# One row-ordered array for attention outputs, and late row tiles on the GpSimd queue, in a kernel of two attention and two gMLP layers

## Chip, cores and metric

The kernel runs on one core of a Trainium2 chip. The metric is device microseconds (us) of one execution; the median of several executions is given. The profile is one more execution, recorded by the hardware profiler.

## What is computed

The input is one sequence of 2048 rows of 512 values in bf16. Four layers follow one another, each adding to the residual `x`: attention, gMLP, attention, gMLP, with the same weights both times.

```python
x = x + _A_ref(_layernorm(x), mem0, Wq, Wk, Wv, Wo, seg_len=32)
x = x + _B_ref(_layernorm(x), w_in, w_sp, b_sp, w_out)
...
# _A_ref: 64 segments of 32 rows, 32 heads of 128, one after the other
h = concat([mem, xs])                  # 8 memory rows and 32 rows
q, k, v = h @ Wq, h @ Wk, h @ Wv       # per head
o = softmax(mask(q @ k.T * scale)) @ v
o = o @ Wo                             # 40 rows of 512
mem = o[:8]; outs.append(o[8:])
...
# _B_ref
z = gelu(x @ w_in)                     # 2048 x 1376
z1, z2 = z[:, :688], layernorm(z[:, 688:])
g = w_sp @ z2 + b_sp[:, None]          # mixes all 2048 rows
return (z1 * g) @ w_out
```

A segment needs the memory rows of the one before it, so attention is a chain of 64 segments. The gMLP works on 16 row tiles of 128 rows; the product with `w_sp` (the gate) needs every row tile.

## The kernel before, in words

**Engines and queues.** TensorE (PE), VectorE (DVE) and ScalarE (ACT) run in the order in which the code names the operations (`ORDERED`, line 28); in the gMLP the same holds for SP, which only issues DMAs (line 216). GpSimd (POOL) and, in attention, SP get their order from the scheduler that builds the program. Every engine's queue is served in order: an instruction that waits holds up those behind it. Each DMA is issued by the queue of one engine.

**Attention** (`a_block`, line 453). `segment` (line 610) projects Q, K and V, forms the scores and the weighted sums, and closes with `wo_pass` (line 547), 128 matmuls into `pw`. `pw` holds 32 rows: the 8 memory rows for the next segment and the first 24 output rows. The last 8 output rows of a segment are computed apart, for 16 segments at once (`wo_last`, line 556; `y_part`, line 565), into `pwB`. So there are two arrays in DRAM: `oA_d` (one slab per segment, written by `store_o`, line 605) and `oB_d` (one slab per 16 segments, line 579 and, after the last segment, line 804). `store_o` runs for all 65 products.

**Rows** (`_Rows`, line 139). When a row tile's attention output is complete, `y_load` (line 172) loads the residual and, by eight small DMAs, the outputs from both arrays; `y_add` (line 185) adds and stores the new residual to `xd`; `y_stats` and `y_norm` (line 193) normalise it and store it as bf16 to `xb_d`. All these stores are on SP's queue. Attention does this for row tiles 0 to 11, one per segment, as soon as they are complete, on DVE. Row tiles 12 to 15 need the last `wo_last`, so the gMLP does them: the late rows. `late_load` (line 239) loads them on POOL's queue and adds on POOL; `late_norm` (line 248) does their statistics and normalising on DVE, with its own Newton steps for the reciprocal root (`_rstd_dve`, line 116: three steps, a dozen tiny operations). `apply` (line 153) prepares a row tile for attention: it normalises, stores to `xn_d`, and loads the result back in eight pieces, on SP's queue.

**gMLP** (`b_block`, line 202). First the projection stage: for each row tile `project` (line 259) runs 12 matmuls of `xnT` (transposed by a DMA from `xb_d`, line 237, three buffers) with `w_in_sb` into one of two PSUM buffers `pz`; ACT takes GELU of both halves (lines 266, 267), DVE the statistics of the second half (269 to 271). After every odd tile DVE does Newton's steps for the pair (line 294), and after the next even tile ACT normalises both (line 274). After tile 5 and tile 9 `late_norm` runs ahead of the pair's Newton steps (line 287), and the loads of tiles 14 and 15 follow tile 5. SP's queue has the transposes of `xnT`, of `w_sp` (three ahead, line 257) and the stores of the late rows.

Then the gate stage, lines 354 to 364: for each output tile `gate` runs 32 matmuls (16 row tiles, two halves) into `pg`, in the same PSUM buffers; `product` (DVE, line 321) multiplies by `z1`; `turn_u` transposes on PE and `finish` multiplies by `w_out`, adds the residual, and in the first gMLP takes the statistics for the next attention and calls `apply` for row tiles 0 and 1. `turn_u` and `finish` of one tile stand inside the gate of the next:

```python
for t in range(NT):
    gate(t, range(0, 6))
    if t > 0:
        turn_u(t - 1)
    gate(t, range(6, 12))
    if t > 0:
        finish(t - 1)
    gate(t, range(12, NT))
    product(t)
```

**Memory.** The pools of a layer lie one behind the other in SBUF in the order of the code, and the next layer's pools take the same addresses: a tile can be written when the tiles that lay there have been read for the last time. In the gMLP `w_in_sb` comes first; at these addresses attention has `hA`, `KA`, `QQ` and `uT`, used until its last segment. `xnT` lies in the pool `b_z` (line 212).

Of the kernel before, what the change touches and what calls it, by code (L numbers as in the profile page):

```python
# [138 lines left out]
class _Rows:  # L139


    def __init__(self, nc, pool, xd, xn_d, xb_d, oA_d, oB_d, x_in):
# [47 lines left out]
    def y_stats(self, tb, MV):  # L190
        _stats(self.nc, self.pool, self.y[tb][0], MV[:, tb, :])

    def y_norm(self, tb, MV, RS):
# [3 lines left out]
        self.nc.vector.tensor_scalar(out=_nat(xn[:]), in0=_perm(o), scalar1=MV[:, tb, 0:1], scalar2=RS[:, tb:tb + 1],
                                     op0=ALU.subtract, op1=ALU.mult)
        self.nc.sync.dma_start(self.xb_d[tb * P:(tb + 1) * P, :], xn[:])


def b_block(tc, c, rows, xd, MV_in, RS_in, MV_out, RS_out, w_in, w_sp, w_out, S, first, out_final=None):
# [641 lines left out]
```

## Time and profile before

| | before |
|---|---|
| median of 3 runs | 1998.38 us (1998.09 to 2000.65) |
| the profiled execution's own time | 1993.78 us |
| span in its trace, first to last instruction | 1992.1 us |
| PE busy | 1787.7 us (90%) |
| DVE busy | 1259.4 us (63%) |
| ACT busy | 1050.9 us (53%) |
| POOL busy | 138.2 us (7%) |
| mean granted clock of PE | 0.97 |

The span lies within the execution's time. Busy times are of the span; matmuls overlap, so a busy PE is not PE at its peak. [...] The first gMLP lies at about 800 to 1018 us, the second at about 1781 to 1992 us.

### The profile page before, as it was taken

To read this page: it belongs to the slowest core of one execution; us is meant where nothing else is said; L and a number is where in the kernel's file an instruction comes from. 1 tells how busy PE (TensorE), PEld (TensorE's weight loads), DVE (VectorE), ACT (ScalarE), POOL (GpSimd) and SP (SyncE) were. 2 spreads that over 40 slices of the span, in tenths; PEclk is the share of its full clock that TensorE was granted. 3 is DMA by queue.
4 is the path that set the end of the run, shared out by engine and by line. 5 is a ranking of instruction groups with operands and counts; after the bars stand their busy time and mean duration, and the time that the engine had idled before them with its cause. 6 is when DMAs were issued, how large, how long until landed. Compare 5 with 4: busy or idle time off the path is not lost.

```text
span 1992.1 us, 94947 instructions
## 1 busy us (share of the span) xinstructions
PE 1787.7 (90%) x43776; PEld 1033.7 (52%) x43776; DVE 1259.4 (63%) x2876; ACT 1050.9 (53%) x1880; POOL 138.2 (7%) x287
## 2 busy tenths in 40 slices
PE   3899999999999999657989999999999999985798
PEld 1555555555555555324645555555555555542355
DVE  2666777777777767353346677667777776665422
ACT  1566666666666665341236666666666666643311
POOL 5000000000000000320010000000000000004000
PEclk8999999999999999878999999999999999997899
DMA  9100000120012001435640000001200210033363
GB/s 348 31 20 18 19 17 17 32 65 26 17 40 64 19 15 47 131 82 123 157 136 24 20 22 20 21 20 57 63 21 24 79 50 15 9 115 100 86 140 101
DMA packets 179935, 120.08 MB, mean 60 GB/s; under 512 B 117280, under 2 KB 156976, under 8 KB 179536
## 3 DMA queue, kind: packets, MB, share of 16 engines
q1 hardware_dynamic: 158864, 70.43, 13.7%
q0 software_dynamic: 9376, 28.88, 4.2%
q10 hardware_dynamic: 11296, 14.70, 2.5%
q8 instruction: 342, 5.60, 1.1%
q14 instruction: 57, 0.47, 0.1%
HBM read 59.29 MB, written 33.69 MB: 47 GB/s over the span
## 4 chain that ended last, share of the span: by engine, by line
PE 39%; DVE 7%; ACT 5%; issue 2%; DMA 2%; POOL 1%; SPq 0%; DVEq 0%; POOLq 0%; ACTq 0%
PE psm L494 12%; PE pg L313 7%; PE pw L551 5%; PE psb L494 4%; DVE KA L631 2%; PE py L338 2%; ACT rows L627 2%; PE psO L674 2%; ACT E L655 2%; PE pwB L560 2%; PE psS L651 1%; DVE E L658 1%; PE psM L718 1%; PE psD L727 1%; PE pT L329 1%
## 5 line engine op out<-in xcount | busy, mean ns | idle before, releaser
L494 PEld LDWEIGHTS <-hA 128*32 128x32 bf16 x12288 | 308.9, 96 | 308.2 <-DVE hA L603 48.5
L627 ACT CAST rows<-psm 128x512 bf16<-128x512 f32 x512 | 300.6, 587 | 189.9 <-PE psm L494 189.9
L551 PE MATMUL pw<-Wo_sb,uT 128*32 128x128 bf16 x16640 | 265.5, 219 | 28.0 <-issue 19.7
L494 PE MATMUL psm<-Wq_sb,hA 128*32 128x512 bf16 x4096 | 273.5, 383 | 13.8 <-DVE hA L603 12.8
L551 PEld LDWEIGHTS <-uT 128*32 128x32 bf16 x16640 | 244.4, 97 | 67.6 <-issue 29.6
L494 PE MATMUL psm<-Wk_sb,hA 128*32 128x512 bf16 x4096 | 270.0, 381 | 0.0
L494 PE MATMUL psv<-Wv_sb,hA 128*32 128x512 bf16 x4096 | 268.2, 382 | 0.0
L631 DVE STREAM_TRANSPOSE QQ<-rows 128x512 bf16<-128x512 bf16 x256 | 182.1, 711 | 89.1 <-ACT rows L627 87.8
L690 DVE TENSOR_TENSOR uT<-psO,Rt 128x384 bf16<-128x384 f32 x256 | 138.1, 539 | 126.1 <-ACT Rt L680 126.1
L631 DVE STREAM_TRANSPOSE KA<-rows 128x512 bf16<-128x512 bf16 x256 | 182.0, 711 | 38.6 <-ACT rows L627 33.1
L655 ACT ACTIVATE E<-psS 128x448 bf16<-128x448 f32 x256 | 140.3, 548 | 107.5 <-PE psS L651 107.5
L637 DVE CAST VA<-psv 128x512 bf16<-128x512 f32 x256 | 175.7, 686 | 2.3 <-PE psv L494 0.2
L313 PE MATMUL pg<-z2n,wspT 128*128 128x344 bf16 x1024 | 164.8, 314 | 12.0 <-ACT z2n L274 7.1
L263 PE MATMUL pz<-w_in_sb,xnT 128*128 128x512 bf16 (+1 forms) x384 | 92.6, 409 | 74.2 <-DMA xnT<-xb_d 53.5
L596 POOL COPY QQ<-QTB 128x256 bf16<-128x256 bf16 x128 | 51.5, 403 | 1408.0 <-PE psS L651 847.1
L651 PEld LDWEIGHTS <-KA 128*64 128x64 bf16 x2048 | 79.8, 113 | 127.9 <-DVE KA L631 127.5
L680 ACT ACTIVATE Rt<-Rt 128x1024 f32<-128x1024 f32 x128 | 135.6, 1059 | 4.0
L313 PEld LDWEIGHTS <-wspT 128*128 128x128 bf16 x1024 | 96.4, 99 | 67.6 <-issue 14.7
L679 ACT ACTIVATE Rt<-psD 128x1024 f32<-128x1024 f32 x128 | 129.0, 1008 | 0.0
L494 PEld LDWEIGHTS <-hB 128*32 128x32 bf16 x3072 | 76.5, 97 | 101.0 <-issue 32.5
L735 DVE TENSOR_TENSOR uT<-psO,Rm 128x128 bf16<-128x128 f32 x256 | 62.8, 286 | 92.5 <-PE psO L674 82.3
L651 PE MATMUL psS<-QQ,KA 128*64 128x80 bf16 x2048 | 109.9, 208 | 10.3
(116 smaller groups left out, 2268.5 us busy)
## 6 DMA issues: line engine op xcount, KB each, us to landing
oA_d<-o_sb SPq DMA_DIRECT2D x130, 64.0 KB
Wo_sb<-in_A_Wo_dram POOLq DMA_DIRECT2D x8, 1024.0 KB, 13.4
xs<-xd ACTq DMA_DIRECT2D x32, 256.0 KB
xd<-y_o SPq DMA_DIRECT2D x28, 256.0 KB
y_o<-oA_d SPq DMA_DIRECT2D x96, 48.0 KB
Wq_sb<-in_A_Wq_dram POOLq DMA_DIRECT2D x8, 512.0 KB, 7.0
Wk_sb<-in_A_Wk_dram POOLq DMA_DIRECT2D x8, 512.0 KB, 11.0
xn_d<-ln_xn SPq DMA_DIRECT2D x32, 128.0 KB
```

Of the source, the lines that this page charges most:

```text
L263: nc.tensor.matmul(pz[:, c0:c1], lhsT=xnT[tt][:, kt, :], rhs=w_in_sb[:, kt, c0:c1], start=(kt == 0), stop=(kt == KT - 1))
L313: nc.tensor.matmul(pg[t][:, k, 0:344], lhsT=wsp[t][:, st, :], rhs=z2n[:, st, 344 * k:344 * k + 344], start=(st == 0), stop=(st == NT - 1))
L494: nc.tensor.matmul(ps[32 * cg:32 * cg + 32, :], lhsT=lhs(kt, cg), rhs=rhs(kt, cg), start=(kt == 0), stop=(kt == KT - 1), tile_position=(0, ...
L551: nc.tensor.matmul(po[32 * cg:32 * cg + 32, 0:128], lhsT=lhs[:, n, :], rhs=wo_rhs(h, cg), start=(h == 0), stop=(h == H - 1), tile_position ...
L627: nc.scalar.copy(r[:], ps[:])
L631: nc.vector.transpose(out=QQ[:, j % 2, :, 0:32] if j < 2 else KA[:, j % 2], in_=r[:])
L637: nc.vector.tensor_copy(VA[:, r].rearrange("p i e -> p (i e)"), ps)
L651: nc.tensor.matmul(pS[64 * g:64 * g + 64, i, c0:80 if K is KA else 112], lhsT=K[:, r, n:n + 2, :].rearrange("p h k -> p (h k)"), rhs=q if ...
L655: nc.scalar.activation(out=E[:, r], in_=pS, func=ACT.Exp, scale=scale)
L679: nc.scalar.activation(out=o, in_=in_, func=ACT.Ln)
L680: nc.scalar.activation(out=o, in_=o, func=ACT.Exp, scale=-1.0)
L690: nc.vector.tensor_tensor(out=hview(uT_nxt, 2 * r, 2 * r + 2, 8, 32), in0=oview(2 * r, 2 * r + 2, 8, 32), in1=Rr[:, :, :, 0:24], op=ALU.mult)
```

## The change

The two arrays become one, `o_d`, whose row M + r (M = 8) is output row r: a segment's product is stored as 32 consecutive rows, the 8 memory rows landing where `store_last` later writes the last 8 output rows of the segment before. `y_load` is then one DMA for the residual and one for the outputs. The product of segment 0 has nothing to store and isn't. In attention the tiles `oB`, `VB`, `KTB` and `QTB` become two fixed buffers each, used in turn, and come first in memory: index 0 of all four, then index 1. In the gMLP `xnT` gets a pool of its own right behind `w_in_sb`; the two together take 14,080 bytes a partition, the four tiles of index 0 take 14,336.

The stores of the late rows, of row tile 11, of the last `o_d` rows and the DMAs of `apply` in the first gMLP are issued on POOL's queue instead of SP's. Tiles 12, 13 and 14 are loaded ahead of the projections and tile 15 after tile 5. The two late tiles share the Newton steps of the projection pair (four columns instead of two and two), after which come their `y_norm`. The gate stage begins with 14 of 16 steps for output tiles 0 and 1, then the last two steps of each; later gates are cut at 8 and 13 instead of 6 and 12.

```diff
     def apply(self, tb, MV, RS, first=False, x=None, eng=None):
+        eng = eng or nc.sync
...
-        nc.sync.dma_start(self.xn_d[M + tb * P:M + (tb + 1) * P, :], xn[:])
+        eng.dma_start(self.xn_d[M + tb * P:M + (tb + 1) * P, :], xn[:])
...
     def y_load(self, tb, first, eng, x=None, o=None):
...
-        ot = o.rearrange("p (cg c) -> p cg c", cg=4)
-        for j in range(4):
-            eng.dma_start(ot[32 * j:32 * j + 24], self.oA_d[4 * tb + j + 1].rearrange("(cg r) c -> r cg c", cg=4)[8:32])
-            r0 = 32 * (tb % 4) + 8 * j
-            eng.dma_start(ot[32 * j + 24:32 * j + 32], self.oB_d[tb // 4, r0:r0 + 8, :].rearrange("r (cg c) -> r cg c", cg=4))
+        eng.dma_start(o, self.o_d[M + tb * P:M + (tb + 1) * P, :])
...
-    def y_add(self, tb, first, eng):
+    def y_add(self, tb, first, eng, store):
...
-        self.nc.sync.dma_start(self.xd[tb * P:(tb + 1) * P, :], o)
+        store.dma_start(self.xd[tb * P:(tb + 1) * P, :], o)
...
         wp = ctx.enter_context(tc.tile_pool(name="b_w", bufs=1))
+        xp = ctx.enter_context(tc.tile_pool(name="b_x", bufs=3))
...
-            xnT[tt] = zp.tile([P, KT, P], BF16, name="xnT", bufs=3)
+            xnT[tt] = xp.tile([P, KT, P], BF16, name="xnT")
...
-            rows.y_add(tb, first, nc.gpsimd)
+            rows.y_add(tb, first, nc.gpsimd, nc.gpsimd)
...
+        def norms(q, late):
+            n = 4 if late else 2
+            for k, tb in enumerate(late):
+                rows.y_stats(tb, mv[q][:, 2 + k, :])
+            rs[q] = zp.tile([P, 4], F32, name="rs")
+            nb[q] = zp.tile([P, 2], F32, name="nb")
+            _rstd_dve(nc, zp, rs[q][:, 0:n], mv[q][:, 0:n, 1], n)
+            nc.vector.scalar_tensor_tensor(out=nb[q][:], in0=mv[q][:, 0:2, 0], scalar=-1.0, in1=rs[q][:, 0:2], op0=ALU.mult, op1=ALU.mult)
+            for k, tb in enumerate(late):
+                rows.y_norm(tb, mv[q][:, 2 + k, 0:1], rs[q][:, 2 + k:3 + k], nc.gpsimd)
...
-        for tb in (NT - 4, NT - 3):
-            late_load(tb)
+        late_load(NT - 4)
+        late_load(NT - 3, gp.tile([P, DM], F32, name="xs")[:], gp.tile([P, DM], F32, name="xo", bufs=1)[:])
+        late_load(NT - 2, gp.tile([P, DM], F32, name="xs")[:], rows.pool.tile([P, DM], F32, name="ln_x")[:])
...
-            if tt in (5, 9):
-                late_norm(NT - 4 + 2 * (tt // 9))
-            if tt == 5:
-                for tb in (NT - 2, NT - 1):
-                    late_load(tb)
...
+                norms(tt // 2, {5: (NT - 4, NT - 3), 9: (NT - 2, NT - 1)}.get(tt, ()))
             elif tt > 1:
                 normalise(tt - 2)
                 normalise(tt - 1)
+            if tt == 5:
+                late_load(NT - 1)
...
-                rows.apply(t, MV_out, RS_out, x=xo[:])
+                rows.apply(t, MV_out, RS_out, x=xo[:], eng=nc.gpsimd)
...
+        gate(0, range(0, NT - 2))
+        gate(1, range(0, NT - 2))
+        gate(0, range(NT - 2, NT))
+        product(0)
+        gate(1, range(NT - 2, NT))
+        turn_u(0)
+        product(1)
+        gate(2, range(0, 6))
+        finish(0)
+        gate(2, range(6, 8))
+        for t in range(2, NT):
+            if t > 2:
+                gate(t, range(0, 8))
+            turn_u(t - 1)
+            gate(t, range(8, 13))
+            finish(t - 1)
+            gate(t, range(13, NT))
             product(t)
...
+        for i in range(2):
+            oBr[i] = pers.tile([P, H, P], BF16, name=f"oB{i}")
+            VBr[i] = pers.tile([P, 2, 4, DH], BF16, name=f"VB{i}")
+            KTBr[i] = pers.tile([P, 2, 16, 32], BF16, name=f"KTB{i}")
+            QTBr[i] = pers.tile([P, 2, 16, 32], BF16, name=f"QTB{i}")
...
+        def store_last(G, eng):
+            eng.dma_start(o_d[M + 512 * G:M + 512 * G + 512, :].rearrange("(j r) d -> j r d", r=32)[:, 24:32, :], yB.pop(G)[:])
...
-            nc.sync.dma_start(oA_d[s], o_sb[:])
+            eng.dma_start(o_d[SEG * (s - 1):SEG * s, :].rearrange("r (cg c) -> cg r c", cg=4), o_sb[:])
...
-            store_o(s, pw)
+            if s > 0:
+                store_o(s, pw, nc.sync)
...
-        store_o(NSEG, pw)
+        store_o(NSEG, pw, nc.gpsimd)
...
-        nc.sync.dma_start(oB_d[NB // 4 - 1], yl[:])
+        store_last(NB // 4 - 1, nc.gpsimd)
...
-        y_add(ys[0])
+        y_add(ys[0], nc.gpsimd)
         run(copies)
-        rows.y_norm(ys[0], MV_out, RS_out)
+        y_norm(ys[0], nc.gpsimd)
```

## Rows read from the trace of the kernel before

**Rows 1.** Windows: us, busy and (count) of PE, PEld, DVE, ACT, POOL; clock; DMA.
```profile
60.00:800.00 740.00, 706.10 (x20406) 417.37 (x20402) 540.32 (x1175) 459.60 (x831) 24.60 (x61) 1.00 0.10 30
811.00:892.50 81.50, 44.89 (x192) 20.43 (x193) 41.19 (x168) 32.75 (x46) 25.86 (x41) 0.77 0.39 100
888.00:892.00 4.00, 4.00 (x22) 1.92 (x20) 2.38 (x12) 3.29 (x5) 0.00 (x0) 1.00 0.66 140
1791.00:1875.00 84.00, 47.34 (x193) 21.27 (x194) 41.84 (x171) 32.73 (x46) 26.18 (x41) 0.74 0.39 98
1895.00:1982.00 87.00, 87.00 (x572) 52.05 (x571) 21.13 (x26) 11.01 (x26) 0.00 (x0) 1.00 0.53 126
```

**Rows 2.** PE's longest wait, 60 to 800 us: total, times, longest.
```profile
PE pw L551 <- issue: 6.4, 16, 0.8
```

**Rows 3.** What PE waited for, 800 to 1020 us: total, times, longest.
```profile
PE pz L263 <- DMA xnT<-xb_d: 26.3, 2, 17.1
PE pz L263 <- ACT z L267: 6.7, 2, 6.1
PE pg L313 <- DMA wspT<-in_B_w_sp_dram: 4.9, 2, 4.2
```

**Rows 4.** Timeline of PE, first gMLP: start, us, line, operation, count, [idle before].
```profile
803.61 7.08 PE L560 MATMUL pwB<-Wo_sb,oB 128*128 128x512 bf16 x32
814.57 8.81 PE L263 MATMUL pz<-w_in_sb,xnT 128*128 128x512 bf16 x36 [3.88 <-issue]
832.67 11.18 PE L263 MATMUL pz<-w_in_sb,xnT 128*128 128x512 bf16 x48 [9.28 <-DMA xnT<-xb_d]
866.34 11.41 PE L263 MATMUL pz<-w_in_sb,xnT 128*128 128x512 bf16 x48 [17.06 <-DMA xnT<-xb_d]
...
1012.04 1.34 PE L313 MATMUL pg<-z2n,wspT 128*128 128x344 bf16 x8
```

**Rows 5.** Timeline of the SP queue, first gMLP.
```profile
829.94 12.81 SPq L237 DMA_TRANSPOSE xnT<-xb_d  x6
...
863.33 0.33 SPq L188 DMA_DIRECT2D xd<-xo  x1
863.75 8.25 SPq L237 DMA_TRANSPOSE xnT<-xb_d  x4
```

**Rows 6.** Timeline of POOL (GpSimd), first gMLP.
```profile
824.07 1.17 POOL L187 TENSOR_TENSOR y_o<-y_o,y_x 128x512 f32<-128x512 f32 x1
...
862.15 1.15 POOL L187 TENSOR_TENSOR xo<-xo,xs 128x512 f32<-128x512 f32 x1 [1.65 <-DMA xo<-oA_d]
```

**Rows 7.** Timeline of ACT (ScalarE), first gMLP.
```profile
810.73 0.59 ACT L803 COPY yB<-pwB 128x512 f32<-128x512 f32 x1 [6.75 <-PE pwB L560]
...
888.55 0.72 ACT L266 ACTIVATE z<-pz 128x688 f32<-128x688 f32 x1
...
892.96 1.81 ACT L274 ACTIVATE z2n<-z,NBz,RSz 128x688 bf16<-128x688 f32 x2 [1.11 <-DVE NBz L295]
894.68 0.72 ACT L266 ACTIVATE z<-pz 128x688 f32<-128x688 f32 x1
```

**Rows 8.** Timeline of DVE (VectorE), first gMLP.
```profile
823.77 1.50 DVE L127 TENSOR_TENSOR nq<-nq,nt 128x2 f32<-128x2 f32 x1
...
845.10 0.70 DVE L135 BATCH_NORM_STATS2 bnst<-y_o 128x6 f32<-128x512 f32 x1
...
847.14 0.17 DVE L119 TENSOR_SCALAR nt<-MV 128x2 f32<-128x2 f32 x1
```

**Rows 9.** DMA issues: count, KB each, median us from issue to landing.
```profile
y_x<-xd POOLq DMA_DIRECT2D x2, 256.0 KB, 3.1
```

**Rows 10.** Timeline of PE, second gMLP.
```profile
1781.60 8.77 PE L560 MATMUL pwB<-Wo_sb,oB 128*128 128x512 bf16 x32
...
1888.79 3.09 PE L313 MATMUL pg<-z2n,wspT 128*128 128x344 bf16 x20
...
1982.91 1.34 PE L313 MATMUL pg<-z2n,wspT 128*128 128x344 bf16 x8
```

More of the change, by code (lines that the diff above doesn't have):

```diff
@@ L177, in y_load, with y_stats, y_norm, b_block @@
         eng.dma_start(x, (self.x_in if first else self.xd)[tb * P:(tb + 1) * P, :])
-        ot = o.rearrange("p (cg c) -> p cg c", cg=4)
-        for j in range(4):
-            eng.dma_start(ot[32 * j:32 * j + 24], self.oA_d[4 * tb + j + 1].rearrange("(cg r) c -> r cg c", cg=4)[8:32])
-            r0 = 32 * (tb % 4) + 8 * j
-            eng.dma_start(ot[32 * j + 24:32 * j + 32], self.oB_d[tb // 4, r0:r0 + 8, :].rearrange("r (cg c) -> r cg c", cg=4))
+        eng.dma_start(o, self.o_d[M + tb * P:M + (tb + 1) * P, :])
         self.y[tb] = (o, x)
-    def y_add(self, tb, first, eng):
+    def y_add(self, tb, first, eng, store):
         o, x = self.y[tb]
         eng.tensor_tensor(out=_perm(o) if first else o, in0=_perm(o) if first else o, in1=_nat(x) if first else x, op=ALU.add)
-        self.nc.sync.dma_start(self.xd[tb * P:(tb + 1) * P, :], o)
-    def y_stats(self, tb, MV):
-        _stats(self.nc, self.pool, self.y[tb][0], MV[:, tb, :])
-    def y_norm(self, tb, MV, RS):
+        store.dma_start(self.xd[tb * P:(tb + 1) * P, :], o)
+    def y_stats(self, tb, mv):
+        _stats(self.nc, self.pool, self.y[tb][0], mv)
+    def y_norm(self, tb, mean, rstd, store):
         o, _ = self.y.pop(tb)
         xn = self.pool.tile([P, DM], BF16, name="ln_xn", bufs=2)
[L197 to L202, printed above, removed]
+        self.nc.vector.tensor_scalar(out=_nat(xn[:]), in0=_perm(o), scalar1=mean, scalar2=rstd, op0=ALU.subtract, op1=ALU.mult)
+        store.dma_start(self.xb_d[tb * P:(tb + 1) * P, :], xn[:])
+def b_block(tc, c, rows, xd, MV_out, RS_out, w_in, w_sp, w_out, S, first, out_final=None):
     nc = tc.nc
@@ L225, in b_block @@
         w_out_sb = mid.tile([P, 6, DM], BF16, name="w_out_sb")
-        MVz = mid.tile([P, NT, 2], F32, name="MVz")
-        RSz = mid.tile([P, NT], F32, name="RSz")
-        NBz = mid.tile([P, NT], F32, name="NBz")
-        xt, xnT, z2, wsp = {}, {}, {}, {}
+        xt, xnT, z2, wsp, mv, rs, nb = {}, {}, {}, {}, {}, {}, {}
         def load_x(tt):
@@ L397 @@
     xb_d = dram.tile([S, DM], BF16, name="xb_d")
-    oA_d = dram.tile([S // SEG + 1, P, P], F32, name="oA_d")
-    oB_d = dram.tile([S // 512, P, DM], F32, name="oB_d")
+    o_d = dram.tile([M + S, DM], F32, name="o_d")
     rp = ctx.enter_context(tc.tile_pool(name="rows", bufs=1))
-    rows = _Rows(nc, rp, xd, xn_d, xb_d, oA_d, oB_d, x_in)
+    rows = _Rows(nc, rp, xd, xn_d, xb_d, o_d, x_in)
     with tc.manual_schedule(engines=ORDERED):
@@ L503, in a_block @@
             nc.gpsimd.memset(t[:], 0.0)
-        oA_d, oB_d, maskM = rows.oA_d, rows.oB_d, c["maskM"]
+        o_d, maskM = rows.o_d, c["maskM"]
         blk_state = {}
@@ L578, in out, with y_add, y_norm @@
                 if q == 3:
-                    nc.sync.dma_start(oB_d[G], yB.pop(G)[:])
+                    store_last(G, nc.sync)
             adds.append(out)
             yield
-        def y_add(tb):
-            rows.y_add(tb, first, nc.vector)
-            rows.y_stats(tb, MV_out)
+        def y_add(tb, store):
+            rows.y_add(tb, first, nc.vector, store)
+            rows.y_stats(tb, MV_out[:, tb, :])
             copies.append(lambda: _rstd_act(nc, RS_out[:, tb:tb + 1], MV_out[:, tb, 1:2], c))
+        def y_norm(tb, store):
+            rows.y_norm(tb, MV_out[:, tb, 0:1], RS_out[:, tb:tb + 1], store)
         seg_state = {}
@@ L618, in segment @@
             if s % 16 == 0:
-                oBs[tb // 4] = blkp.tile([P, H, P], BF16, name="oB")
+                oBs[tb // 4] = oBr[tb // 4 % 2]
             oB = oBs[tb // 4]
@@ L786, in tail @@
                 if ys:
-                    rows.y_norm(ys.pop(0), MV_out, RS_out)
+                    y_norm(ys.pop(0), nc.sync)
                 if tb % 4 == 3 and j4 == 0 and tb > 4:
```

56 lines of the change are left out of this document (18 added, 38 removed).

## The prediction

> **What bounds the kernel now.** I read the windows first, then who waits for whom, then the timelines of single engines around the places where TensorE (PE) stands still. In the attention blocks PE is busy 706.1 of 740 us at full clock [rows 1]; the longest entry in its waits there is 6.4 us, in pieces under 1 us, and none ends on a DMA [rows 2]. The last part of each gMLP is as dense: 87.0 of 87 us [rows 1]. Between them lies the projection stage (16 row tiles, 12 matmuls each). There PE is busy 44.9 of 81.5 us in the first gMLP and 47.3 of 84 in the second, at mean granted clocks of 0.77 and 0.74 [rows 1]. So some 165 us of 1992 are badly used, and nearly all that the change can win lies there and at its two ends. The list of waits names what PE lacks: 26.3 us on transposed inputs `xnT`, 6.7 on its PSUM buffers (which ScalarE empties), 4.9 on `wspT` [rows 3]. The timeline has the same as holes: 3.88 us ahead of the first projection, 9.28 ahead of the fourth tile, 17.06 ahead of the tenth [rows 4]. SP's own timeline gives the reason: the transposes stand in its queue behind the store `xd<-xo` of a late row tile and leave 0.4 us after it, at 863.75 [rows 5]. That store waits for GpSimd's add, which started at 862.15 after a wait for its loads [rows 6]. Tiles that have nothing to do with the late rows are held up by queue order alone.
>
> **What limits the stage once SP is free.** Two row tiles then form a loop: ScalarE's GELU of the odd tile, VectorE's statistics and Newton steps, ScalarE's two normalisations, the next odd tile. The undisturbed pair runs from 888.55 to 894.68: 6.13 us, of which 4.41 to the first normalisation [rows 7]. PE's work for a tile is 8x512 + 4x352 = 5504 columns; at the 0.221 us per 512 columns of the product before it (7.08 us for 32) [rows 4] that is 2.38 us, 4.76 us for a pair. So PE fits in at full clock, which it had from 888 to 892 [rows 1] while this loop ran.
>
> **The change, part by part.**
> First weights and `xnT` over dead tiles, last read in segment 60 of 0 to 63. Both can land before attention ends. The first projection then needs only the PSUM of the last product, free when ScalarE's copy ends, 810.73 + 0.59 = 811.32 [rows 7]. First GELU: 811.32 + 2.38 = 813.7, since the product leaves the clock full.
> Stores of late rows on GpSimd's queue. SP keeps transposes alone: the 9.28 and 17.06 us go. Late next is the loop of pairs: GELU of tile 1 at 813.7 + 2.38 = 816.1, and seven pairs of 6.13 us bring tile 15 to 859.0.
> Newton shared. Each of the two late pairs still lays its statistics on the loop, 845.10 to 847.14 = 2.04 us [rows 8], 4.1 in all, but no second chain of Newton steps. Their normalising passes follow it, beside ScalarE's normalisations: nothing. So 863.1.
> GpSimd's adds stay. The one at 824.07 took 1.17 us [rows 6], and a 2-element VectorE operation over it took 1.50 us [rows 8]. Four a block cost from 0 to 4 x 1.2 = 4.8 us, according to how many meet Newton steps; I take two, 2.4 us, as three of them follow close on each other at the first steps: tile 15 at 865.5. [...]
> GpSimd's queue now holds the last output store, the two stores of tile 11, two `w_out` loads, 8 late loads instead of 36, 4 adds, 8 late stores; in the first gMLP also the 18 DMAs that prepare the next attention's first two tiles, ahead of its `Wo` loads. Only late rows and that preparation stand behind its waiting instructions. A load of 256 KB lands in 3.1 us [rows 9], taken for the stores too. The last output, copied at 811.3, can be read at 815; three loads and adds end at about 823, and statistics want tile 12 at 830. Tile 15 (buffers free at 835, two stores and two loads issued at 0.6 each, 3.1, 1.2) is ready at 842, wanted at 845. Tile 14's input is tight: normalising 0.7, store 0.6 + 3.1, transpose 2.6 (863.75 [rows 5] to the matmul at 866.34 [rows 4]), 7.0 us, against 1.8 + 6.13 + 1.3 - 2.4 = 6.8 until PE wants it. Cost 0 to 2 us; I take 0, because 3.1 is for twice a bf16 tile's bytes.
> Gate order. Fourteen of the sixteen steps of the first two gates now come before the last two normalisations are needed: 28/32 of two gates at 6.72 - 1.74 = 4.98 (below), 8.7 us of PE work. Tile 15 is normalised 4.41 + 1.81 us after its GELU starts [rows 7], so it is covered; without that cover up to 6 us a block would return. The first gate starts with the last GELU, or up to 6.13 - 1.4 - 2.38 = 2.4 us ahead of it: I take 1, so 864.5.
> Gate stage. From the second gate's end to the last one's are 14 periods, 1982.91 - 1888.79 [rows 10], 6.72 us each. Sixteen, less the one turn and output product that the first lacks (3840 of 14848 columns, 1.74 us), plus 0.5 for a first product on VectorE, are 106.3 us. The `wspT` waits go, since 9 DMAs for each of the next attention's first tiles leave SP.
> Output array. Nine loads a tile become two, 130 small stores 128. SP gives up time that PE never waited for: nothing, bounded by 3 us either way. Fixed buffers, the store left out, small statistics tiles: nothing, they stand beside PE's 95% in attention.
>
> **The sum.** First gMLP: the last gate ends at 864.5 + 106.3 = 970.8 instead of 1012.04 + 1.34 = 1013.4 [rows 4]: 42.6 us. Second: the product ends at 1781.60 + 8.77 = 1790.4; copy 0.6, then 2.4 to the first GELU, 51.8 to the last (2.4 + 42.9 + 4.1 + 2.4), less 1, and 106.3 bring the last gate to 1950.5 instead of 1984.25 [rows 10]: 33.8 us, as its gates had run without waits. Together 76.4. The profiled execution took 1993.78 us, 1.7 more than its span; 1917.4 follows. The median shown, 1998.38, lies 4.6 above that execution, so I forecast **1922 us**.
>
> **Rivals.**
> *Late rows still come late.* GpSimd's queue is served in order; a store of tile 12 behind a waiting load, or slower landings, would hold `xnT` of tiles 14 and 15. For: no slack at tile 14. Against: tiles 12, 13 and 15 have 3 us or more. A hole like the 9.28 us one a block: about 10, so 1942. [...]
> *PE stays at the lower clock.* For: means of 0.74 and 0.77 [rows 1]. Against: the long holes explain them, and 888 to 892 has 1.00. A tile would take 4.76 us, the stage 76 instead of 53: 23 us a block lost, 1968.
> *The early loads are not early.* If `w_in` and `xnT` stay behind the end of attention in their queues, the first projection starts as now: about 5 us a block, 1932.
> *Slower.* The single array joins stores and wide loads in SP's queue: a segment's store waits for a load of rows, a load for the last store, and the `pre` inputs behind them arrive late. It decides from 76/128 = 0.6 us a segment; at 0.8 us the time is 1922 + 102 = 2024. Against: fewer instructions in that queue, and no PE wait on it now [rows 2].
>
> **From this to the numbers.** Forecast 0.70, late rows 0.13, low clock 0.08, loads not early 0.06, slower 0.03. A time within 0.2% (4 us, about what a measurement of this kernel tells from no change) needs gains and losses that cancel: 0.01, out of the forecast's share. Low end: no add blocks (-4.8), gates start early (-2.8), the median lies no higher than the profiled execution (-4.6), SP gives 3: 1907. High end: every add blocks (+4.8) and the late rows' case: 1946. Low clock, slower and the tails lie outside.
>
> **What would show it.** Right: no PE hole above 2 us between the last output product and the first gate; odd GELUs 6.1 us apart, about 8 where late statistics stand; clock 1.00 there; the first projection within 1 us of ScalarE's copy; no PE wait on `wspT`; attention as long as before. Wrong: holes on `xnT` at tiles 12 to 15 (late rows), matmuls at twice the time (clock), longer segments with PE waiting for `hA` (slower).

## The result, and the profile after

The changed kernel takes **1941.3 us** (1934.49 to 1941.62, 4 runs) against 1999.14 of the kernel before on the same chip: ratio 0.9702, 95% interval 0.968 to 0.9724. That is 58 us off. It is faster, as forecast, and lies inside the range, but some 20 us above the 1922 forecast. The profiled execution took 1941.53 us with a span of 1939.8.

The stages, read off the timelines of PE and ScalarE (us; first gMLP / second; "product" is the last attention output product `pwB`):

| stage | before | forecast | after |
|---|---|---|---|
| product's end to first GELU | 7.59 / 8.57 | 3.0 / 3.0 | 13.28 / 14.19 |
| first to last GELU (16 tiles) | 76.40 / 77.68 | 51.8 / 51.8 | 50.86 / 51.08 |
| last GELU to first gate | -2.15 / -1.65 | -1.0 / -1.0 | -1.10 / -1.45 |
| gates | 120.85 / 109.28 | 106.3 / 106.3 | 111.65 / 106.30 |
| product's end to last gate | 202.69 / 193.88 | 160.1 / 160.1 | 174.69 / 170.12 |
| second attention | 777.0 | 777.0 | 775.8 |

So 51.8 us of the 76.4 came. The missing 24.6 us stand in two rows: the first GELU is 10.3 and 11.2 us later than forecast, and the first gMLP's gates are 5.35 us longer; that is 26.8 us, and the other rows give 2.2 us back.

PE in the first gMLP (timeline; compare [rows 4]):

```profile
804.21 7.08 PE L569 MATMUL pwB<-Wo_sb,oB 128*128 128x512 bf16 x32
818.21 1.86 PE L245 MATMUL pz<-w_in_sb,xnT 128*128 128x512 bf16 x4 [6.92 <-DMA w_in_sb<-in_B_w_in_dram]
821.49 13.09 PE L245 MATMUL pz<-w_in_sb,xnT 128*128 128x512 bf16 x56 [1.42 <-DMA w_in_sb<-in_B_w_in_dram]
835.59 4.81 PE L245 MATMUL pz<-w_in_sb,xnT 128*128 128x512 bf16 x24 [1.01 <-ACT z L249]
...
849.62 6.49 PE L245 MATMUL pz<-w_in_sb,xnT 128*128 128x512 bf16 x24 [3.10 <-ACT z L249]
```

In the second gMLP it is the same (compare [rows 10]):

```profile
1754.65 7.08 PE L569 MATMUL pwB<-Wo_sb,oB 128*128 128x512 bf16 x32
1768.47 1.86 PE L245 MATMUL pz<-w_in_sb,xnT 128*128 128x512 bf16 x4 [6.74 <-DMA w_in_sb<-in_B_w_in_dram]
1772.85 11.25 PE L245 MATMUL pz<-w_in_sb,xnT 128*128 128x512 bf16 x44 [2.51 <-DMA w_in_sb<-in_B_w_in_dram]
```

What PE waited for, 800 to 1020 us (compare [rows 3]):

```profile
PE pz L245 <- ACT z L249: 9.0, 5, 3.1
PE pz L245 <- DMA w_in_sb<-in_B_w_in_dram: 8.3, 2, 6.9
PE pT L322 <- DVE u L314: 6.3, 6, 1.9
```

The holes on `xnT` of 9.28 and 17.06 us are gone; PE now waits for ScalarE, as the forecast's loop of pairs (GELU, statistics and normalising of two row tiles) wants. In the second gMLP two small ones are left, of 1.43 and 0.74 us. The hole ahead of the first projection has grown from 3.88 to 6.92 us, and has another releaser: the weights. GpSimd's timeline says why:

```profile
807.66 0.73 POOL L621 DMA_DIRECT2D o_d<-o_sb  x1
811.87 0.79 POOL L218 DMA_DIRECT2D w_in_sb<-in_B_w_in_dram  x1 [3.48 <-issue]
812.65 0.55 POOL L563 DMA_DIRECT2D o_d<-yB  x1
813.22 0.56 POOL L195 DMA_DIRECT2D xb_d<-ln_xn  x1
813.77 0.78 POOL L219 DMA_DIRECT2D w_in_sb<-in_B_w_in_dram  x1
...
851.29 1.15 POOL L184 TENSOR_TENSOR y_o<-y_o,y_x 128x512 f32<-128x512 f32 x1 [2.47 <-DMA y_o<-o_d]
```

The weights leave right behind the last product's end (811.29), not ahead of it; in the kernel before the two halves left at 804.24 and 804.99. The windows (columns as in [rows 1]) show what follows, and that the second gMLP's gates are as forecast:

```profile
811.00:876.00 65.00, 47.66 (x206) 21.80 (x205) 37.49 (x149) 34.92 (x49) 16.79 (x25) 0.84 0.54 142
816.00:826.00 10.00, 6.37 (x17) 2.31 (x18) 0.66 (x2) 1.38 (x2) 5.24 (x8) 0.50 1.03 335
1845.00:1925.00 80.00, 80.00 (x526) 47.69 (x524) 18.89 (x24) 10.16 (x24) 0.00 (x0) 1.00 0.53 132
```

After 6.92 us of idling the granted clock is 0.50 (1.00 is full) from 816 to 826, so the first tile costs twice its 2.38 us on top of the late loads. The 10.3 us of the first gMLP are 6.3 of a later first matmul, 1.4 of waiting for the second half of the weights, and 2.6 of lower clock. The clock fell again behind the two waits of 3.10 us: behind the first, 24 matmuls took 6.49 us instead of 4.81, and behind the second it was 0.50 from 864 to 868 us. The second gMLP's gates run at 80.00 of 80 us.

GELUs of odd tiles on ScalarE (tiles 5, 7, 11, 13, 15; compare [rows 7]):

```profile
840.31 0.72 ACT L248 ACTIVATE z<-pz 128x688 f32<-128x688 f32 x1
...
848.21 0.72 ACT L248 ACTIVATE z<-pz 128x688 f32<-128x688 f32 x1
...
863.10 0.72 ACT L248 ACTIVATE z<-pz 128x688 f32<-128x688 f32 x1
...
869.29 0.74 ACT L248 ACTIVATE z<-pz 128x688 f32<-128x688 f32 x1
...
875.43 0.72 ACT L248 ACTIVATE z<-pz 128x688 f32<-128x688 f32 x1
```

Undisturbed pairs take 6.19 and 6.14 us, the pair with late statistics 7.90: forecast 6.13 and 8.17.

### The profile page after: what moved, and what is told of

Its sections match the earlier page's. It is cut to its first block, busy times and chain, and to the rows that moved or that the text cites. A ratio compares the mean times of both kernels' runs of the same rounds, so it can differ in the third digit from the quotient of the medians.

```text
span 1939.8 us, 94543 instructions
## 1 busy us (share of the span) xinstructions
PE 1782.6 (92%) x43776; PEld 1031.1 (53%) x43776; DVE 1247.4 (64%) x2828; ACT 1047.8 (54%) x1878; POOL 131.0 (7%) x273
## 3 DMA queue, kind: packets, MB, share of 16 engines
q1 hardware_dynamic: 143528, 65.11, 13.4%
## 4 chain that ended last, share of the span: by engine, by line
PE 66%; DVE 13%; ACT 12%; issue 4%; DMA 4%; SPq 1%; POOL 0%; DVEq 0%; POOLq 0%; ACTq 0%
PE psm L503 23%; PE pw L557 10%; PE psb L503 8%; PE pg L306 7%; DVE KA L644 5%; ACT rows L640 4%; ACT E L668 4%; PE psO L687 3%; PE psS L664 3%; PE pwB L569 3%; DVE E L671 3%; PE py L331 2%; PE psM L731 2%; PE psD L740 2%; PE pz L245 1%
## 5 line engine op out<-in xcount | busy, mean ns | idle before, releaser
L503 PE MATMUL psm<-Wq_sb,hA 128*32 128x512 bf16 x4096 | 275.2, 384 | 13.3 <-DVE hA L615 12.3
L306 PE MATMUL pg<-z2n,wspT 128*128 128x344 bf16 x1024 | 160.1, 310 | 0.0
L608 POOL COPY QQ<-QTB 128x256 bf16<-128x256 bf16 x128 | 51.5, 403 | 1407.6 <-PE psS L664 846.0
L306 PEld LDWEIGHTS <-wspT 128*128 128x128 bf16 x1024 | 95.3, 98 | 52.2 <-issue 6.8
## 6 DMA issues: line engine op xcount, KB each, us to landing
Wv_sb<-in_A_Wv_dram POOLq DMA_DIRECT2D x8, 512.0 KB, 11.2
```

The costliest lines, as they stand in the source:

```text
L306: nc.tensor.matmul(pg[t][:, k, 0:344], lhsT=wsp[t][:, st, :], rhs=z2n[:, st, 344 * k:344 * k + 344], start=(st == 0), stop=(st == NT - 1))
L503: nc.tensor.matmul(ps[32 * cg:32 * cg + 32, :], lhsT=lhs(kt, cg), rhs=rhs(kt, cg), start=(kt == 0), stop=(kt == KT - 1), tile_position=(0, ...
```

## The experiments

One table for all (medians differ a little between groups of runs, so compare ratios to the kernel before; stages in us from the profile, first gMLP / second; "first GELU" is counted from the product's end, "loop" is first to last GELU, "att. 1 ends" is the first product's end, "att. 2" the second attention):

| kernel | ratio, interval | first GELU | loop | gates | att. 1 ends | att. 2 |
|---|---|---|---|---|---|---|
| before | 1 | 7.6 / 8.6 | 76.4 / 77.7 | 120.9 / 109.3 | 810.7 | 777.0 |
| after | 0.9702, 0.968-0.9724 | 13.3 / 14.2 | 50.9 / 51.1 | 111.7 / 106.3 | 811.3 | 775.8 |
| e1 | 0.9696, 0.9682-0.971 | 3.2 / 3.2 | 51.4 / 52.1 | 109.5 / 106.3 | 820.8 | 786.4 |
| e2 | 0.9705, 0.9691-0.9719 | 12.4 / 12.9 | 51.5 / 52.6 | 113.2 / 106.3 | 809.3 | 778.6 |
| e3 | 0.972, 0.9704-0.9735 | 12.9 / 14.5 | 51.0 / 52.6 | 111.5 / 106.3 | 813.4 | 781.6 |
| e4 | 0.9753, 0.9733-0.9773 | 13.1 / 13.9 | 50.9 / 51.1 | 114.8 / 110.3 | 810.4 | 779.1 |
| e5 | 0.9767, 0.9745-0.9789 | 12.9 / 14.1 | 55.5 / 57.5 | 109.7 / 106.3 | 808.4 | 779.0 |
| e6 | 0.9789, 0.9769-0.9809 | 13.3 / 13.4 | 57.5 / 60.2 | 112.9 / 106.3 | 814.5 | 781.5 |
| e7 | 0.9897, 0.9878-0.9916 | 10.4 / 10.0 | 64.1 / 66.5 | 122.0 / 109.3 | 811.4 | 778.8 |
| e9 | 0.9626, 0.9609-0.9644 | 3.2 / 3.2 | 51.4 / 52.2 | 111.9 / 107.0 | 813.9 | 779.4 |
| e10 | 0.9673, 0.9649-0.9697 | 3.2 / 3.2 | 51.6 / 51.4 | 110.1 / 106.3 | 816.0 | 784.8 |
| e11 | 0.9736, 0.971-0.9763 | 13.5 / 13.7 | 51.1 / 51.8 | 115.7 / 106.3 | 808.5 | 776.9 |
| e12 | 0.9685, 0.966-0.971 | 3.2 / 3.2 | 51.4 / 50.8 | 119.1 / 106.3 | 816.1 | 780.2 |
| e14 | 0.9605, 0.9585-0.9625 | 3.2 / 3.2 | 51.5 / 52.2 | 107.4 / 106.3 | 812.3 | 777.5 |

Kernels whose attention is the same instruction for instruction (after, e4, e5, e6, e11) end their first product between 808.4 and 814.5 us and spend 775.8 to 781.5 us in the second attention. Differences of this size there are not read as effects of an edit unless a row names the wait.

### Why the first weights are late: e1, e10, e9, e2

In the built program of the kernel after, `w_in_sb` lies over index-0 attention tiles alone, last read in segment 60, yet its load waits for the last matmul of the last product, which reads `oB1`. Both are tiles of one pool. A pool is a group of tiles that the program reserves and gives back together. Theory: a tile laid over a released pool waits for the last reader of the whole pool. In e1, e9 and e10 the index-0 tiles get a pool of their own; `w_in_sb` keeps the very same address. e9 adds `hA0` to that pool (last read in segment 62), e10 both `hA` tiles (segment 63):

```diff
-        pers = ctx.enter_context(tc.tile_pool(name="a_pers", bufs=1))
+        first_pool = ctx.enter_context(tc.tile_pool(name="a_first", bufs=1))
...
         for i in range(2):
+            pers = first_pool if i == 0 else ctx.enter_context(tc.tile_pool(name="a_pers", bufs=1))
...
-        hA = [pers.tile([P, KT, 32], BF16, name=f"hA{i}") for i in range(2)]
+        hA = [(first_pool, pers)[i].tile([P, KT, 32], BF16, name=f"hA{i}") for i in range(2)]
```

(The last two lines are e9's; e10 takes `first_pool` for both, e1 leaves them.)

> The change with one difference: the four tiles of index 0 get a pool of their own instead of sharing one with index 1, hA, KA, QQ and uT; the addresses stay. Theory (whole pool): in the changed kernel the first weights are issued only after the last product pwB, 0.6 us behind its end, because a tile laid over a pool waits for the last reader of the whole pool, and that is pwB reading oB1. With a pool of their own the loads of w_in should be issued around segment 61, more than 20 us ahead, and the first GELU should start 3 us after the product's end in both gMLPs instead of 13.3 and 14.2 us: 21 us less, 1920 us (1917 to 1924). Rival (queue order): the loads stand at the end of attention in GpSimd's and SP's queues whatever memory they take; then nothing moves, 1941. Rival (something else holds the first GELU, such as the table load or the work on row tile 11): loads early, gain under 5 us, 1936 or more.

**e1** measured 1939.3 us (1934.46 to 1940.35), no gain over the kernel after that its interval tells, with the first GELU 3.2 us behind the product in both gMLPs: the theory holds, and a new wait took the gain. Timelines of POOL, SP and VectorE of e1:

```profile
767.85 0.76 POOL L218 DMA_DIRECT2D w_in_sb<-in_B_w_in_dram  x1 [6.19 <-PE pwB L570]
```
```profile
767.60 3.48 SPq L231 DMA_TRANSPOSE xnT<-xb_d  x2
771.17 0.56 SPq L564 DMA_DIRECT2D o_d<-yB  x1
771.79 2.25 SPq L231 DMA_TRANSPOSE xnT<-xb_d  x1
780.21 0.35 SPq L179 DMA_DIRECT2D y_o<-o_d  x1
```
```profile
783.18 0.69 DVE L184 TENSOR_TENSOR y_o<-y_o,y_x 128x512 f32<-128x512 f32 x1 [7.51 <-DMA y_o<-o_d]
```

The transposes stand on SP ahead of the store of `yB` (the last output rows of segments 32 to 47, ready in segment 60); the load of row tile 8 that reads it leaves at 780.21, VectorE waits 7.51 us for it, and PE with it. Queue order is the smaller part of this: the store left 3.3 us later than in the kernel after (771.17 for 767.84), and the load 9.0 us behind the store, where it is 2.8 in the kernel after, with the DMA engines 0.87 to 1.06 busy from 768 to 780 us. The first attention grows by 9.5 us, the second by 10.6.

> The kernel after, with the index-0 attention tiles and both hA tiles in a pool of their own, so that the weights and xnT that lie over this pool wait for segment 63's last v product instead of the last attention product (and not for segment 60's, as in e1_own_pool). Theory (the late first weights are the shortfall, and e1 lost its gain to the early transfers standing ahead of segment 60's stores): the loads go out around 797 to 800 us, land before the last product ends at 811, the first GELU comes 3.2 us after that product in both blocks instead of 13.3 and 14.2, attention 2 stays at 776 us, and no wait of PE for hA appears: 10.1 + 11.0 = 21.1 us less than 1941.3, so 1920 us (1917 to 1925). Rival (1.4 MB of weights beside running attention costs what it gives back wherever it stands): first GELU at 3.2 us, but attention longer by 7 to 10 us in each block, 1936 to 1941.

**e10** measured 1933.1 us (1928.91 to 1935.56): neither number. The waits for `hA` are those of the kernel after (1.9 us in all), but there is this on PE (timeline), and its clock (windows):

```profile
800.19 1.97 PE L558 MATMUL pw<-Wo_sb,uT 128*32 128x128 bf16 x128 [1.17 <-issue]
806.40 0.29 PE L558 MATMUL pw<-Wo_sb,uT 128*32 128x128 bf16 x2 [4.24 <-issue]
806.63 9.32 PE L570 MATMUL pwB<-Wo_sb,oB 128*128 128x512 bf16 x32
```
```profile
802.00:804.00 2.00, 0.16 (x12) 0.02 (x1) 0.00 (x0) 0.00 (x0) 0.00 (x0) 1.00 1.31 235
804.00:806.00 2.00, 0.00 (x0) 0.00 (x0) 0.00 (x0) 0.00 (x0) 0.00 (x0) 0.59 0.62 220
```

Ahead of the last `pw` matmuls PE stands for 4.24 us where it stood 1.77 in the kernel after and 1.50 before, with the weights in flight (DMA share 1.31 from 802 to 804); the clock then falls (0.59 from 804 to 806) and the last product takes 9.32 us instead of 7.08. With 0.6 us at the stop before (1.17 for 0.53), that is 2.5 + 0.6 + 2.2 = 5.3 us of attention; the second block has the same stop, at 4.0 us. The profile names no releaser; the last section has what the packets say. The second attention also began at a granted clock of 0.89 (1000 to 1030 us; 1.00 in the kernel after), and why is open.

> As e10_late_own_pool, but only the first hA tile is in the pool of the index-0 tiles, so that the first weights and xnT wait for segment 62's last v product, one segment earlier. Theory (a transfer of 1.4 MB beside attention costs only where something on the path needs the DMA engines at that time: segment 60's stores and loads in e1, in e10 the last two products of the last pw, which stood 4.2 us where they stand 1.8 us in the kernel after): in segment 62 the load of row tile 10 is issued some 7 us before its add, the weights are in by about 793, the wait at the last pw is back at 1.5 to 1.8 us, TensorE's clock stays at its upper level, the first GELU is 3.2 us behind the last product in both blocks: 1920 us (1917 to 1926). Rival (it costs what it gives back wherever it stands): a wait of 5 us or more for hA, uT or at pw in segments 62 and 63, 1930 to 1938.

**e9** measured 1926.3 us (1924.77 to 1928.78), at the upper end of the theory's range. The weights leave at 786.19, between the two places that cost:

```profile
786.19 0.76 POOL L218 DMA_DIRECT2D w_in_sb<-in_B_w_in_dram  x1 [12.26 <-PE psM L733]
```
```profile
PE pw L558 <- issue: 2.5, 2, 1.8
```

The stop at the last `pw` is back at 1.8 us (second fence: waits of PE, 760 to 825 us), and no wait for `hA` is longer than in the kernel after. The theory holds for the most part. The attentions are 2.6 and 3.6 us longer than in the kernel after, which is inside what kernels with one and the same attention differ by. One step of it can be read: from one `y_add` to the next across the loads are 12.76 us instead of 11.24, and 1.1 us of that is a stop of PE without a releaser, like that of e10. That this is what is missing to 1920 is not shown.

> The change with the memory of the kernel before: KTB, QTB, VB and oB rotate in the pool a_blk again, xnT lies in b_z. Theory (whole pool): w_in lies over hA, KA, QQ and uT, whose pool ends with the last wo_pass, some 7 us ahead of the product's end; xnT lies elsewhere and waits for the product. So w_in lands before the product ends, the first GELU starts 7.5 us after its end as in the kernel before, and the memory part of the change by itself has cost time: 5.8 and 6.7 us less than the change, 1929 us (1926 to 1932). Rival (queue order): the position in the queue decides, first GELU 13 us after the product as in the change, 1941.

**e2** puts `oB`, `VB`, `KTB`, `QTB` back into `blkp` with its two buffers and `xnT` into `zp`, the memory of the kernel before:

```diff
-            xnT[tt] = xp.tile([P, KT, P], BF16, name="xnT")
+            xnT[tt] = zp.tile([P, KT, P], BF16, name="xnT", bufs=3)
...
-                oBs[tb // 4] = oBr[tb // 4 % 2]
+                oBs[tb // 4] = blkp.tile([P, H, P], BF16, name="oB")
```

1940.17 us (1936.73 to 1943.47), where 1929 was expected. The weights do leave ahead of the product's end (805.15 and 806.61), but now the inputs are last (timeline of PE):

```profile
816.97 9.20 PE L244 MATMUL pz<-w_in_sb,xnT 128*128 128x512 bf16 x31 [7.64 <-DMA xnT<-xb_d]
```

The transposes can leave only behind the product (809.36), while weights and late rows are still landing (DMA share 1.07 from 811 to 816). So "first weights over dead tiles", as made, is worth nothing, and the layout before would have been no better.

### The parts that made the gain: e7, e6, e5, e4

> The kernel before, with the attention outputs in one array in row order alone. My forecast costs this part at nothing on the path: 1998 us within 0.2%. Rival (it is this that shortens the late rows: on GpSimd one load of 256 KB stands where five to eight issues stood, 0.5 to 0.7 us each, so late rows come some 4 to 5 us earlier and the second hole of 17 us shrinks by that in each block): 1986 to 1990 us, with the first hole unchanged.

**e7** is the kernel before with one output array:

```diff
-        for j in range(4):
-            eng.dma_start(ot[32 * j:32 * j + 24], self.oA_d[4 * tb + j + 1].rearrange("(cg r) c -> r cg c", cg=4)[8:32])
...
-            eng.dma_start(ot[32 * j + 24:32 * j + 32], self.oB_d[tb // 4, r0:r0 + 8, :].rearrange("r (cg c) -> r cg c", cg=4))
+        eng.dma_start(o, self.o_d[M + tb * P:M + (tb + 1) * P, :])
```

1981.83 us (1976.59 to 1983.8), ratio 0.9897: some 20 us faster by itself by the medians, 15 between the two profiled executions. My forecast for this part, nothing, is refuted. Both holes are shorter (timelines of SP and PE; [rows 4 to 6] have the same places of before):

```profile
854.85 0.33 SPq L184 DMA_DIRECT2D xd<-xo  x1
855.27 8.44 SPq L233 DMA_TRANSPOSE xnT<-xb_d  x4
```
```profile
831.64 10.94 PE L259 MATMUL pz<-w_in_sb,xnT 128*128 128x512 bf16 x47 [5.23 <-DMA xnT<-xb_d]
...
858.11 11.35 PE L259 MATMUL pz<-w_in_sb,xnT 128*128 128x512 bf16 x47 [10.11 <-DMA xnT<-xb_d]
```

GpSimd issues one load for a late row tile's outputs instead of eight, so the last add of the second group starts at 853.68 instead of 862.15, the store leaves SP 8.5 us earlier, and the transposes with it. The first hole is another matter: its row tile starts only 1.0 us earlier (831.64 for 832.67), and the hole is 4.05 us shorter mostly because PE comes to it later, the first GELU being 2.8 us later. There the rival, which had the first hole unchanged, is nearly right. The loop is 12.3 and 11.2 us shorter; from the product's end to the last GELU it is 9.5 and 9.7.

> The kernel after, with the stores of the late row tiles (their sum and their normalised rows) back on the SP queue, among the xnT transposes. Theory of the forecast (the queue alone removes both holes of [rows 4], 9.28 and 17.06 us): the pair loop grows by about 26 us in each block, 1941.3 + 52 = 1994 us. Rival (the holes were long because each late row came from many small loads of two arrays and was added late; in the kernel after the adds end at 830 and 852 us, and SP would stand only until then): an xnT late by 2 to 3 us at tiles 3 and 9 and by 1 us at tile 12, some 5 us a block, about 1951 us (1946 to 1958).

**e6**: 1961.05 us (1956.61 to 1966.1).

```diff
-            rows.y_add(tb, first, nc.gpsimd, nc.gpsimd)
+            rows.y_add(tb, first, nc.gpsimd, nc.sync)
...
-                rows.y_norm(tb, mv[q][:, 2 + k, 0:1], rs[q][:, 2 + k:3 + k], nc.gpsimd)
+                rows.y_norm(tb, mv[q][:, 2 + k, 0:1], rs[q][:, 2 + k:3 + k], nc.sync)
```

Between the two, nearer to the rival. Holes come back at tiles 3, 9 and 13, of 2.58, 8.35 and 2.81 us (SP, then PE):

```profile
856.90 0.33 SPq L185 DMA_DIRECT2D xd<-y_o  x1
857.32 8.78 SPq L231 DMA_TRANSPOSE xnT<-xb_d  x4
```
```profile
835.31 11.03 PE L245 MATMUL pz<-w_in_sb,xnT 128*128 128x512 bf16 x47 [2.58 <-DMA xnT<-xb_d]
...
860.10 12.26 PE L245 MATMUL pz<-w_in_sb,xnT 128*128 128x512 bf16 x47 [8.35 <-DMA xnT<-xb_d]
...
875.18 8.83 PE L245 MATMUL pz<-w_in_sb,xnT 128*128 128x512 bf16 x36 [2.81 <-DMA xnT<-xb_d]
```

The queue is worth 6.6 and 9.1 us of loop, not 26.3: with one array the rows are in time for a shorter hold.

> The kernel after, with a Newton chain of its own for the two late rows in the four late pairs (12 more DVE instructions each, 2.25 us by the chain from 844.06 to 846.30 us). Theory (in a pair with late rows DVE is the bound, so sharing the chain is worth its whole length): the four late pairs grow from 7.9 to 10.1 us, 1941.3 + 9 = 1950 us (1948 to 1952). Rival (the chain hides in the idle time of DVE behind ACT and PE): 1941 to 1944.

```diff
-            _rstd_dve(nc, zp, rs[q][:, 0:n], mv[q][:, 0:n, 1], n)
+            if late:
+                _rstd_dve(nc, zp, rs[q][:, 2:4], mv[q][:, 2:4, 1], 2)
+            _rstd_dve(nc, zp, rs[q][:, 0:2], mv[q][:, 0:2, 1], 2)
```

**e5**: 1951.77 us (1950.76 to 1952.45); the late pairs, two in each block, take 10.0 us instead of 7.9, and the loops grow by 4.7 and 6.4 us (2.0 of the 6.4 in the pair from tile 3 to 5, which the edit does not touch). The theory holds: VectorE is the bound of a late pair, and a shared chain is worth its length.

> The change with the gate loop of the kernel before (one gate after the other, cuts at 6 and 12). Theory: PE waits for the last two normalisations again, 3 to 4 us in each gMLP, and runs some matmuls at the lower clock after it: 8 us more, 1949 (1946 to 1953). Rival: the normalisations are in time by now or the order costs elsewhere as much as it gives: 1941.

```diff
-        gate(0, range(0, NT - 2))
-        gate(1, range(0, NT - 2))
-        gate(0, range(NT - 2, NT))
...
+        for t in range(NT):
+            gate(t, range(0, 6))
+            if t > 0:
+                turn_u(t - 1)
...
```

**e4** has the gate loop of the kernel before: 1950.7 us (1943.21 to 1954.14). Its waits of PE, 860 to 990 us, hold what the new order covers:

```profile
PE pg L306 <- ACT z2n L270: 3.7, 2, 3.3
```

2.9 us of the same stand in the second gMLP. The stage sums rise by 2.0 and 3.5 us; the rest of the 10 us lies in an attention that the edit does not touch, so its price is 5 to 10 us.

As shares of the kernel before: array 1.03 (e7), queue 0.87 (e6), Newton 0.65 (e5), gate order 0.51 (e4), memory 0.03% (e2): 3.09 against the 2.98% of the whole. Each ratio has an interval of 0.14 to 0.22 either way, and the array was put into the kernel before while the others were taken out of the kernel after, so the sum agrees loosely. The earlier load of tile 14 was not tried apart.

### The first gMLP's gates: e3, e11, e12, e14

In the kernel after VectorE's add waits for the residual rows, which were issued on ScalarE's queue at 901.93:

```profile
909.36 0.69 DVE L340 TENSOR_TENSOR xo<-py,xs 128x512 f32<-128x512 f32 x1 [6.98 <-DMA xs<-xd]
```

> The change with the preparation of the next attention's first two row tiles (18 DMAs in the first gMLP) back on SP's queue. Theory: on GpSimd's queue its small DMAs ran beside the transposes of w_sp and made the residual loads xs land 7 us after their issue, so that VectorE and then PE waited about 4.4 us in the first gate stage; on SP the transposes of w_sp wait instead, 4.9 us in the kernel before. About equal: 1941 (1938 to 1945), with the waits moved from u to wspT. Rival (the forecast's): the queue change was worth the whole 4.9 us, 1946 or more. Second rival: with more gate work ahead SP's stop is covered, 1937 or less.

```diff
-                rows.apply(t, MV_out, RS_out, x=xo[:], eng=nc.gpsimd)
+                rows.apply(t, MV_out, RS_out, x=xo[:])
```

**e3** gives the apply's transfers back to SP: 1942.92 us (1940.21 to 1948.83). The waits for `xs` fall from 27.5 us to 13.7, a wait of 1.9 us for `wspT` comes in, behind which 16 gate matmuls take 4.15 us (clock 0.83 from 910 to 920 us), and the gates stay at 111.5. The wait only changes its name.

> The kernel after, with the residual rows xs of a gate tile loaded one period earlier (after the add that frees the buffer, the first two ahead of the gates). Theory (in the first gMLP the residual load stands behind the transposes of w_sp and the apply's small transfers, and DVE's add waits for it, 5.3 us in all): the waits of DVE's add for xs go, the first block's gates fall from 111.65 to 106.3 us as in the second, whose gates stay: 1941.3 - 5.3 = 1936 us (1933 to 1939). Rival (the transfers' capacity is the bound in this stretch, so another load is late instead): a wait of PE for wspT or of DVE's adds stays, the gates stay at 110 to 112 us, 1941.

```diff
-            load_x(t)
...
             nc.vector.tensor_tensor(out=_perm(xo[:]), in0=_nat(py[:]), in1=_perm(xs[:]), op=ALU.add)
+            if t + 2 < NT:
+                load_x(t + 2)
```

**e11** (with `load_x(0)` and `load_x(1)` ahead of the gates): 1945.14 us (1937.86 to 1951.04). The theory falls: 115.7 us of gates. Waits of VectorE, 870 to 990 us:

```profile
DVE xo L341 <- DMA xd<-xo: 22.7, 4, 9.3
```

The add no longer waits for its input but for the store of the sum before, which must leave the one buffer `xo`.

> Both edits of e10_late_own_pool and e11_early_residual. If the two causes are separate and both theories hold, the sum: 1941.3 - 21.1 - 5.3 = 1915 us (1911 to 1920), which is what my forecast for the change itself would be with the terms that failed set right. If the loads early in the block make the residual loads late again, only the first: 1920.

**e12** (e10 and e11 together): 1935.1 us (1931.24 to 1938.84), gates 119.1. The two edits do not add.

> e9_mid_own_pool, with the residual rows loaded one period earlier and two buffers for the gate tile's sum xo, so that neither the load of xs nor the store of xo can hold DVE's add within a period. It is read by the gate stage of the first gMLP. Theory (from e11, where the wait only moved from the load to the store: the DMA engines are the bound while the apply's transfers, the w_sp transposes and the float32 rows run together): the gates stay at 110 to 119 us with waits for wspT or still for xs, and the kernel is no faster than e9. Rival (what is missing is only room in time for one transfer): 106.3 us as in the second gMLP, and 4 to 5 us less than e9, so about 1915.

```diff
-            xo = gp.tile([P, DM], F32, name="xo", bufs=1)
+            xo = gp.tile([P, DM], F32, name="xo", bufs=2)
```

**e14** is e9 with e11's loads and this second buffer: **1922.39 us** (1918.77 to 1925.64), ratio 0.9605 with an interval clear of the kernel after's: the best version. Waits of VectorE, 870 to 990 us:

```profile
DVE xo L341 <- PE py L330: 62.5, 16, 4.3
```

All sixteen adds wait for PE alone, the gates take 107.4 us where e9 has 111.9, and the rival's mechanism holds: what was missing was time for one transfer, not capacity. Its 1915 was not reached, as it counted from the 1920 expected of e9; by the ratios' intervals e14 and e9 are not told apart, and the second buffer without the earlier loads was not tried. Stage sums are 159.8 and 159.9 us where the forecast has 160.1 for each.

## Why the prediction was right and wrong

**Sign and size.** Right: the loss of before was in the projections, and 51.8 of 76.4 us came back in the two gMLPs. The medians tell the same: 1998.4 against 1922 forecast is 76, 58 measured. The 1922 has 4.6 us for a median above the profiled execution; in the kernel after the profiled execution stands at the median (1941.53 and 1941.3), so the 4.6 did not come, and the 1917.4 that the stages gave missed by 24. That the time lies inside the range is partly luck: its high end was put together from late rows and from every add blocking, and neither came. With the two steps set right (e14) the profiled execution took 1918.77.

**First weights and `xnT` over dead tiles: this step failed.** "Both can land before attention ends" took the overwritten bytes' last reader for what the load waits for; the paragraph on memory ahead of the prediction says the same and is wrong in it. The program waits for the pool's: same address, and the load leaves at 811.87, 795.83, 786.19 or 767.85 us with the tiles that share its pool. I had this as a rival ("the early loads are not early") at 0.06 and 5 us a block, so 1932; it cost 10.3 and 11.2, because the load left later than before (811.87 for 804.24), and because PE's clock fell over the idling. My 2.38 us for the first tile hung on "the product leaves the clock full"; the row from 816 to 826 has 0.50.

**Gate stage.** 106.3 us was exact in the second gMLP. In the first it was 5.35 short: the `wspT` waits went, as forecast, but the residual loads became late in their place (27.5 us of VectorE's waits, none in e14), and I had not asked what else lands there.

**Loop of pairs.** Total right within a microsecond (50.9 and 51.1 for 51.8), attribution wrong. "The 9.28 and 17.06 us go" was put down to the queue alone and the array at "nothing": e7 gives the array 9.5 and 9.7 us a block from the product's end to the last GELU, e6 the queue 6.6 and 9.1 of loop. I priced the array on SP, where nobody waits, though I counted on GpSimd "8 late loads instead of 36", whose end the store on SP waits for.

**Newton, adds, gate order.** Late pairs 7.90 for 8.17; one add over a Newton step costs 0.86 us:

```profile
851.43 1.02 DVE L127 TENSOR_TENSOR nq<-nq,nt 128x2 f32<-128x2 f32 x1
```

Its neighbours take 0.16 us; GpSimd's add stood from 851.29 to 852.44, and the operation ended with it at 852.45; why is not shown. The pairs from tile 1 to 3 and 7 to 9 took 6.54 and 6.98 us, 1.3 us in all where I took 2.4. The adds cost less than the 2.4 because the loop came 10 us late, when the first three were all but over. In e14, where it starts in time, two adds end to end (825.70 to 827.98) hold one VectorE operation for 2.02 us where others of its kind take 0.17:

```profile
825.99 2.02 DVE L119 TENSOR_SCALAR nt<-mv 128x2 f32<-128x2 f32 x1
```

The two pairs that meet adds take 7.97 and 6.98 us there, 2.7 in all, and 3.3 in the second gMLP: the term was about right for the loop that it was meant for. First gate 1.1 us ahead of the last GELU, for 1.

**Rivals and signs.** Late rows were in time (GpSimd's queue issued each of their stores in 0.53 to 0.58 us), the clock was low only behind the idling (0.50 behind PE's waits of 6.92 and 3.10 us), attention was no longer: these three are out. The 4.76 us a tile of the low-clock rival are twice 2.38, as at a clock of 0.50: the kernel before has it from 866 to 870 us, where 9 matmuls keep PE busy for 3.66 us. Of the signs of being right, "no PE hole above 2 us" could not hold beside a late pair of 8.17 us with 4.76 us of PE work: two waits of 3.10 us came, "clock 1.00" failed behind them, and neither lengthened a pair.

## What to carry to other kernels

A tile laid over dead memory is loaded when the dependency is released, not when the bytes are dead (here at 767.85 to 811.87 us for one address): look up what the load waits for, and group tiles in pools by their last reader. Then choose the release: an early 1.4 MB can cost what it saves (in e1 the attentions grew by 9.5 and 10.6 us), and one segment earlier or later decided here between 1939, 1926 and 1933 us. When freeing a wait only renames it (load, `wspT`, store), give the chain a second buffer before blaming bandwidth (e14: 107.4 us of gates for 111.9).

## What the runs showed of the hardware that I had not expected

PE stops ahead of the last `pw` matmuls with no releaser in the profile, for 1.5 to 1.9 us in the kernels before and after and for 4.0 to 4.5 us where 1.4 MB were in flight (e10 and e12). The traces suggest that it waits for its instructions. In the kernel after one DMA queue is marked as carrying instructions (q8; DMA queues of the whole execution: packets, MB, share):

```profile
q8 instruction: 342, 5.60, 1.2%
```

These are 342 packets of 16,384 bytes, and PE ran 87,552 matmuls and weight loads, 256 for each packet. The stop of e10 ends at 806.40, 2.66 us behind the start of such a packet (803.74), that of the kernel after at 804.05, 2.59 us behind one (801.46). Over all fourteen traces 363 of the 365 stops above 0.4 us that have no releaser end 2.2 to 3.0 us behind the start of one; of the stops with a named releaser in the kernel after, 4 of 62 do (from 50 us on). Ahead of the stop at the last `pw` the packet starts 5.8 to 6.1 us behind the one before it in e10 and e12, 3.5 to 4.0 in the kernels before and after. No run changed the instructions to try it.

Transposes filled the DMA engines more than plain copies did, 51.8% against 23.0% from 936 to 950 us of the kernel after (DMA queues: packets, MB, share of 16 engines' span; q1 carries two `w_sp` transposes, q10 ScalarE's loads and stores):

```profile
q1 hardware_dynamic: 4161, 1.05, 51.8%
q10 hardware_dynamic: 574, 1.05, 23.0%
```

The same 1.05 MB took 2.25 times the engine time, in packets of 0.25 KB against 1.8 KB. The share may hold time in which packets wait for one another, and how fast a transpose lands by itself no run here tells.
